# One MLP kernel: blocks of 256 or 320 tokens within a batch instead of blocks of 512 tokens across batches

## The chip, the cores and the metric

The kernel runs on one core of a Trainium2 chip. The metric is the device time of one execution in microseconds (us). Before the change the median of three runs is 1290.62 us (1290.39 to 1291.06).

## The reference

For 8 batches of 576 tokens and 8 heads of 64, an attention over 32 memory slots is followed by two MLP blocks, all in float32:

```
a    = softmax(phi, over the 576 tokens)          # phi: (8, 8, 576, 32)
k_m  = a^T k ;  v_m = a^T v                       # per batch and head: (32, 64)
x    = softmax(q k_m^T / 8) v_m                   # heads joined: (8, 576, 512)
x    = x + relu(layernorm(x) * g1 @ w1) @ w2      # w1: (512, 2048), w2: (2048, 512)
h    = gelu(x @ w_in);  u, v = halves of h        # w_in: (512, 1024)
v_s  = w_sg @ (layernorm(v) * g2) + b_sg          # mixes the 576 tokens of a batch
out  = x + (u * v_s) @ w_out                      # w_out: (512, 512)
```

w1, w2, w_in and w_out arrive as 64-bit words that are converted on the chip.

## The kernel before, in words

Two batches form a pair of 1152 tokens, that is 9 tiles of 128; tile 4 of a pair holds the last 64 tokens of its even batch and the last 64 of its odd batch (`tile_rows`). There are 36 tiles.

**Phase 1** computes attention and the first MLP. Because x is a product of attention weights (256 of them per token) and v_m, the kernel folds w1 into the values: for each batch b and each part fb of 512 of the 2048 hidden columns, `make_vw` (line 507) multiplies the batch's v_m with the centred, scaled w1 (`WC`, read back from a scratch in HBM by `load_wc`) and splits the result into a high and a low float32r half, VW[b, fb]: two tiles of 4 KB per partition. So the weights of the first matmul differ from batch to batch. The attention of a tile (`lay_q`, `load_q`, `t_q`, `t_scores`, `t_norm`, `t_attn`) ends with the transposed attention weights in aT, again as high and low halves; `t_x` computes x itself for the residual, `t_ln` its statistics. Before a batch's first tile come its `load_phi`, `load_kv`, and the `prep_` functions.

The MLP runs over 9 blocks of 512 tokens (4 tiles), each in 16 chunks c of 128 hidden columns; one step is one block and chunk. `m1` (line 549) multiplies VW with aT into the PSUM tile ph: six matmuls (two row halves times high-high, high-low and low-high) for each piece of the block that belongs to one batch (`pieces`, line 537). relu goes by ScalarE (hh, line 563) and VectorE (the low half hl, line 564), on all 512 columns at once. `m2` (line 567) multiplies hh and hl of each of the four tiles with W2[c], three matmuls of 512 columns per tile, accumulated over the 16 chunks in four PSUM banks; LAG = 2 steps lie between m1 and m2. The last block takes its chunks in the order 12 to 15, 0 to 11.

The rest of phase 1 is placed by an event list: `at_time(time, function, ...)` with times in steps (16 per block, `tile_base` for tiles), negative ones before the first step; `run_until` calls what is due in the middle and at the end of a step. The framework's scheduler starts from this program order when it orders each engine's queue. Nearly all DMAs are issued by SyncE in one queue (line 80).

Buffers: wpool has 22 slots of 4 KB per partition (raw weights, the 16 final W2, some VW, later the weights of phase 2, the normalised v tiles vhl and, for pair 0, scratch), wpool2 has 13 (wc and the other VW). ph has two PSUM banks, the y of m2 four, attention two.

**Phase 2** is the second MLP, per pair. Its beginning is laid beside the last block's 16 steps by `begin_phase2(n)`: w_sg, w_in and w_out are loaded and split, `y_in` reads pair 0's tiles back transposed, and `s2` (v half, its gelu and layer norm, into vhl) runs for tiles 0 to 4. Then `phase2` runs `s3` (u half), `s4` (mixing over tokens, pvs), and `s5` (output) in 16 units per pair, with `s2` of pair 0's remaining tiles and of the next pair between them.

Of the kernel before, what the change touches and what calls it, by code (L numbers as in the profile page):

```python
# [28 lines left out]
def fused_kernel(ctx: ExitStack, tc: tile.TileContext, q, k, v, phi, g1, w1, w2, w_in, g2, w_sg, b_sg, w_out, out):  # L29
# [7 lines left out]
    P = 128  # L37
# [6 lines left out]
    B1, F1 = 9.2, 0.5  # L44
    HK = H * NM // P
    BLK = TB * P
    NB = B * S // BLK
    REM = S - 4 * P
    SCALE = 1.0 / math.sqrt(D)
# [23 lines left out]
    wpool = ctx.enter_context(tc.tile_pool(name="wpool", bufs=22))  # L73
# [61 lines left out]
    def phase1():  # L135
        R["mo"] = mo = pool(es_mlp, "mo", 2)
        ps_h = pool(es_mlp, "ps_h", 2, space=PSUM)
        ps_y = pool(es_mlp, "ps_y", 1, space=PSUM)
        at = pool(es_attn, "at", 1, side="right")
        at2 = pool(es_attn, "at2", 2, side="right")  # L140
        ps_a = pool(es_attn, "ps_a", 2, space=PSUM, side="right")
        wpool2 = pool(es_w2, "wpool2", 13)
# [25 lines left out]
        def load_phi(b, gs):  # L168
            if gs[0] == 0:
                st["phi"] = (  # L170
# [3 lines left out]
            ph, pr = st["phi"]  # L174
# [5 lines left out]
        def load_kv(b, g, part):  # L180
            n = 3 * g + part
            if b == 0 and n >= 3:
                t = wpool.tile([P, 2, 4, 2, D], F32, tag="w", name="kv")
            else:
                t = at2.tile([P, 2, 4, 2, D], F32, tag="kv", name="kv", bufs=3)
# [10 lines left out]
            st["kv", g, part] = t  # L196
# [11 lines left out]
        def load_q(u, b, i):  # L208
            n = u["n"]
            if u["T"]["t"] < TB:  # L210
                if i % 2 == 0:
                    st["q0"] = two(wpool, F32, "q0")
                t = st["q0"][i % 2].rearrange("p (h d) -> p h d", h=H)
                load(t, q[b, :, i * P:(i + 1) * P, :].rearrange("h p d -> p h d"))
# [7 lines left out]
        def prep_max(b, gs):  # L222
            ph, pr = st["phi"]
# [14 lines left out]
            st["dg"] = dg  # L238

        def prep_exp(b, gs):  # L240
            ph, pr = st["phi"]
            n, hs = len(gs), slice(4 * gs[0], 4 * gs[-1] + 4)
            mb = ps_of(b, [P, 4 * n, NM], "mb")
            PE.matmul(mb.rearrange("p h m -> p (h m)"), ones, st["dg"].rearrange("p g n -> p (g n)"), start=True, stop=True)
# [5 lines left out]
        def prep_sum(b):  # L250
            ph, pr = st["phi"]
# [12 lines left out]
            st["rs"] = rs  # L264

        def prep_kv(b, g, part):
            ph, pr = st["phi"]
            if (g, part) == (0, 0):
                st["kvp"] = ps_a.tile([P, 2, 2 * D], F32, tag="a", name="kvp")
            kvp = st["kvp"]  # L270
            t = st.pop(("kv", g, part))
# [30 lines left out]
        def prep_kT(b):  # L302
            kvn = st["kvn"]
# [33 lines left out]
        def t_scores(u):  # L337
            n, kT = u["n"], st["kT"]
# [643 lines left out]
```

## Time and profile before

| | |
|---|---|
| median of three runs | 1290.62 us (1290.39 to 1291.06) |
| span of the profiled execution, first to last instruction | 1287.4 us |
| TensorE busy | 1230.4 us |
| VectorE busy | 679.6 us |
| ScalarE busy | 440.6 us |
| GpSimd busy | 408.6 us |
| mean granted clock of TensorE, share of full speed | 0.981 |

The profile is of one execution, and gives no time of its own for it beside the span; the median of the runs is 3.2 us above the span. "Busy" counts the time in which an engine has at least one instruction in work; matmuls overlap each other, so the cost of one is read from the distance between starts and not from its own duration.

### The profile page before, as it was taken

The page shows a single profiled execution, that of the slowest core. Times are in us where ns is not written, and L with a number is a line of the kernel's source. Part 1 is how long each engine was busy: PE and PEld are TensorE (multiplying, and loading weights), DVE is VectorE, ACT ScalarE, POOL GpSimd, SP SyncE. Part 2 cuts the span into 40 slices and gives each one's busy share as a digit, 9 for nine tenths or more (in the row PEclk, how much of TensorE's full clock was granted, in tenths as well). Part 3 has the DMA queues.
Part 4 walks back from the last instruction along what each step waited for, and adds up shares of the span by engine and source line. Part 5 has one row for each costly group of instructions (what it writes and reads, how often), then busy time and mean ns, then how long its engine had stood idle before and what let it go on. Part 6 is the DMA issues. An engine that isn't in the chain of part 4 may idle for free.

```text
span 1287.4 us, 20559 instructions
## 1 busy us (share of the span) xinstructions
PE 1230.4 (96%) x7723; PEld 1024.8 (80%) x7723; DVE 679.6 (53%) x1472; ACT 440.6 (34%) x870; POOL 408.6 (32%) x659
## 2 busy tenths in 40 slices
PE   4589989999999999999999999999999999999998
PEld 2367667888878888788787888778998998998997
DVE  3677564445355355345354434765567547547632
ACT  2653332222223232132132123543353444434430
POOL 1144222111102111111021112514575666647641
PEclk8689989999999999999999999999999999999999
DMA  9996673164353453532431104322033024013301
GB/s 213 305 259 162 188 189 91 52 182 123 100 146 99 117 142 89 146 106 79 136 83 58 51 25 136 123 84 75 25 91 106 1 80 134 9 34 115 91 9 66
DMA packets 205076, 138.96 MB, mean 108 GB/s; under 512 B 95536, under 2 KB 176688, under 8 KB 204976
## 3 DMA queue, kind: packets, MB, share of 16 engines
q1 hardware_dynamic: 204976, 137.64, 38.4%
q8 instruction: 61, 1.00, 0.3%
q14 instruction: 39, 0.32, 0.1%
HBM read 114.53 MB, written 31.46 MB: 113 GB/s over the span
## 4 chain that ended last, share of the span: by engine, by line
PE 84%; DMA 7%; DVE 4%; SPq 2%; issue 1%; ACT 1%; POOL 1%; POOLq 0%; DVEq 0%; ACTq 0%
PE ph L559 17%; PE py L574 9%; PE py L576 9%; PE pvs L891 9%; PE py L575 9%; PE po L914 8%; PE pu L866 7%; PE pv L794 6%; DMA raw<-in_moe_w_ch_dram 4%; PE pvw L515 2%; PE sc L342 2%; SPq L80 2%; PE kvp L276 1%; DMA kv<-in_v_dram 1%; PE px L452 1%
## 5 line engine op out<-in xcount | busy, mean ns | idle before, releaser
L559 PE MATMUL ph<-aTh,vw 128*128 128x64 f32 (+7 forms) x1024 | 254.1, 318 | 10.2 <-ACT aTh L410 4.6
L574 PE MATMUL py<-whl,hh 128*128 128x512 f32 x576 | 230.3, 403 | 0.0
L575 PE MATMUL py<-whl,hh 128*128 128x512 f32 x576 | 227.5, 395 | 0.0
L576 PE MATMUL py<-whl,hl 128*128 128x512 f32 x576 | 225.6, 395 | 0.0
L559 PEld LDWEIGHTS ph<-aTh,vw 128*128 128x128 f32 x1024 | 178.2, 191 | 33.3 <-issue 7.5
L564 DVE SCALAR_TENSOR_TENSOR hl<-ph,hh 128x512 fp32r<-128x512 f32 x144 | 99.0, 687 | 169.8 <-ACT hh L563 169.5
L563 ACT ACTIVATE hh<-ph 128x512 fp32r<-128x512 f32 x144 | 86.0, 599 | 266.2 <-PE ph L559 264.9
L559 PE MATMUL ph<-aTl,vw 128*128 128x448 f32 (+7 forms) x512 | 163.7, 320 | 0.0
L574 PEld LDWEIGHTS py<-whl,hh 128*128 128x128 f32 x576 | 108.6, 188 | 30.0 <-issue 6.3
L576 PEld LDWEIGHTS py<-whl,hl 128*128 128x128 f32 x576 | 108.3, 188 | 27.9 <-issue 5.1
L421 POOL TENSOR_TENSOR z<-z,r 128x256 f32<-128x256 f32 (+1 forms) x36 | 20.5, 570 | 342.7 <-DVE r L420 278.7
L575 PEld LDWEIGHTS py<-whl,hh 128*128 128x128 f32 x576 | 108.6, 189 | 20.9 <-issue 2.1
L891 PE MATMUL pvs<-wsh,vhl 128*128 128x288 f32 x576 | 121.2, 294 | 0.0
L559 PEld LDWEIGHTS ph<-aTl,vw 128*128 128x128 f32 x512 | 97.7, 191 | 16.0 <-issue 8.6
L866 PE MATMUL pu<-yTh,whl 128*128 128x288 f32 x512 | 110.4, 295 | 0.0
L794 PE MATMUL pv<-whl,yTh 128*128 128x512 f32 x288 | 91.9, 400 | 3.8 <-DVE vg L784 3.8
L891 PEld LDWEIGHTS pvs<-wsh,vhl 128*128 128x128 f32 x576 | 94.3, 188 | 0.6
L914 PE MATMUL po<-whl,gh 128*128 128x512 f32 x288 | 90.8, 391 | 0.0
L866 PEld LDWEIGHTS pu<-yTh,whl 128*128 128x128 f32 x512 | 85.0, 188 | 1.0
L866 PE MATMUL pu<-yTl,whl 128*128 128x288 f32 x256 | 75.4, 295 | 0.0
L891 PE MATMUL pvs<-wsl,vhl 128*128 128x288 f32 x256 | 75.4, 295 | 0.0
L894 POOL TENSOR_TENSOR gt<-gt,ug 128x288 f32<-128x288 f32 x64 | 51.6, 808 | 63.7 <-DVE gt L893 62.8
(161 smaller groups left out, 2079.0 us busy)
## 6 DMA issues: line engine op xcount, KB each, us to landing
wc<-w_d SPq DMA_DIRECT2D x56, 512.0 KB, 4.9
y_d<-x SPq DMA_DIRECT2D x36, 256.0 KB, 3.9
yr<-y_d SPq DMA_DIRECT2D x36, 256.0 KB, 3.0
kv<-in_k_dram SPq DMA_DIRECT2D x32, 256.0 KB, 4.3
kv<-in_v_dram SPq DMA_DIRECT2D x32, 256.0 KB, 4.4
raw<-in_moe_w_ch_dram SPq DMA_DIRECT2D x32, 256.0 KB, 9.6
raw<-in_moe_w_ch_dram SPq DMA_DIRECT2D x16, 512.0 KB, 8.2
out_dram<-yr SPq DMA_DIRECT2D x32, 256.0 KB, 2.0
```

The source lines that it names most:

```text
L80: return nc.sync.dma_start(out=out_ap, in_=in_ap)
L559: PE.matmul(ph[:, c0:c1], w[:, ks], x[:, g, c0:c1], start=(n == 0), stop=(n == 3 * HK - 1))
L563: A.activation(hh, ph, AF.Relu)
L564: st["hl"] = V.scalar_tensor_tensor(out=hl, in0=ph, scalar=0.0, in1=hh.bitcast(F32), op0=ALU.max, op1=ALU.subtract)
L574: PE.matmul(py, hh[:, ts_], wh, start=start, stop=False)
L575: PE.matmul(py, hh[:, ts_], wl, start=False, stop=False)
L576: PE.matmul(py, hl[:, ts_], wh, start=False, stop=stop)
L794: PE.matmul(pv, y[:, kc, cs], w, start=(n == 0), stop=(n == 3 * KC - 1))
L866: PE.matmul(pu, w[:, ds_], y[:, kc, cs], start=(n == 0), stop=(n == 3 * KC - 1))
L891: PE.matmul(pvs, v_, w_, start=(n == 0), stop=(n == len(ops) - 1))
L894: G.tensor_tensor(out=gt, in0=gt, in1=ug, op=ALU.mult)
L914: PE.matmul(po, gg[:, dc, cs], w, start=(n == 0), stop=(n == 3 * KC - 1))
```

## The change

- **Blocks.** There are 16 blocks within a batch instead of 9 across batches. An even batch has a block of 256 tokens and then one of 320, an odd batch one of 320 and then one of 256. Every m1 is one piece of six matmuls.
- **Carry.** relu's result for an even batch's last 64 tokens is stored per chunk in a carry tile (16 of them); the odd batch's first block puts its own tokens of tile 4 beside them, and m2 takes that full tile there. relu of a 320-token block is two instructions on each engine instead of one, 64 and 256 columns.
- **Order.** Batch 0 goes part by part of w1 through both blocks; the last batch goes chunk by chunk through both; all others finish one block and then the other. Times in the event list count 18 per batch. LAG is 3 of the shorter steps, and hh and hl have four buffers.
- **Event times.** All tile times and those of W1, W2, `make_vw` and `load_wc` are new.
- **Buffers.** wpool has 19 slots; VW rotates over five places of two tiles; wc has four tiles; kv two instead of three; x seven instead of eight; aT three. In phase 2, vhl of tiles 7 and 8 goes to a new pool w3, and pv has one bank until phase 2 (tile 35's y takes the other).
- **Batch 0's fifth group.** The 64 tokens of tile 4 go through the same functions as the first four tiles, as a third group.

```
-    B1, F1 = 9.2, 0.5
+    F1 = 0.5
...
+    BW = 2 * P + REM
+    VQ = 5
+    VMAIN = (4, 0)
+    VTAIL = 2 * (VQ - len(VMAIN))
+    LAG = 3
...
-    wpool = ctx.enter_context(tc.tile_pool(name="wpool", bufs=22))
+    wpool = ctx.enter_context(tc.tile_pool(name="wpool", bufs=19))
...
+        crp = pool(es_mlp, "crp", 1)
...
-        wpool2 = pool(es_w2, "wpool2", 13)
+        vmain = pool(es_mlp, "vmain", 2 * len(VMAIN))
+        tail = pool(es_w2, "tail", 1)
...
-                t = at2.tile([P, 2, 4, 2, D], F32, tag="kv", name="kv", bufs=3)
+                t = at2.tile([P, 2, 4, 2, D], F32, tag="kv", name="kv")
...
+        def aT_of(j):
+            if j not in aT:
+                aT[j] = tuple(mo.tile([P, HK, BW], F32R, tag=f"aT{n}", name=f"aT{n}", bufs=3) for n in "hl")
+            return aT[j]
...
+        def t_x(u, b):
+            T, o, n = u["T"], u["o"], u["n"]
...
+        def wc_tiles():
+            return [tail.tile([P, 2, DM], F32, tag="wc", name="wc", bufs=4) for _ in range(2)]
...
-                h, l = two(wpool if b % 2 and fb < NFB - 1 else wpool2, F32R, "vw")
+                q_ = (NFB * b + fb) % VQ
+                if q_ in VMAIN:
+                    t = vmain.tile([P, 2, DM], F32R, tag="w", name="vw")
+                else:
+                    t = tail.tile([P, 2, DM], F32R, tag="vw", name="vw", bufs=VTAIL)
...
+        blocks = []
+        for b in range(B):
+            w = 18 * b
+            if b % 2 == 0:
+                blocks += [(b, 0, 2 * P, w, 8), (b, 2 * P, S, w + 8, 10)]
+            else:
+                blocks += [(b, 0, 2 * P + REM, w, 10), (b, 2 * P + REM, S, w + 10, 8)]
...
+        def relu(out_h, out_l, src):
+            A.activation(out_h, src, AF.Relu)
+            return V.scalar_tensor_tensor(out=out_l, in0=src, scalar=0.0, in1=out_h.bitcast(F32), op0=ALU.max, op1=ALU.subtract)
...
         def m1(j, c):
...
-            ph = ps_h.tile([P, BLK], F32, tag="h", name="ph")
-            for c0, c1, b in pieces(j):
-                n = 0
-                for g in range(HK):
-                    wh, wl = VW[b, fb][g]
-                    for w, x in ((wh, ah), (wh, al), (wl, ah)):
-                        PE.matmul(ph[:, c0:c1], w[:, ks], x[:, g, c0:c1], start=(n == 0), stop=(n == 3 * HK - 1))
...
+            ph = ps_h.tile([P, BW], F32, tag="h", name="ph")[:, 0:w]
+            n = 0
+            for g in range(HK):
+                wh, wl = VW[b, fb][g]
+                for w_, x in ((wh, ah), (wh, al), (wl, ah)):
+                    PE.matmul(ph, w_[:, ks], x[:, g, 0:w], start=(n == 0), stop=(n == 3 * HK - 1))
+                    n += 1
+            hh = mo.tile([P, 2 * P], F32R, tag="hh", name="hh", bufs=LAG + 1)
+            hl = mo.tile([P, 2 * P], F32R, tag="hl", name="hl", bufs=LAG + 1)
+            o = 0
+            if w > 2 * P:
+                if b % 2 == 0:
+                    carry[c] = crp.tile([P, 2, P], F32R, tag=f"cr{c}", name="cr")
+                    cs, ps = slice(0, REM), slice(2 * P, w)
+                else:
+                    cs, ps = slice(REM, P), slice(0, REM)
+                    o = REM
+                relu(carry[c][:, 0, cs], carry[c][:, 1, cs], ph[:, ps])
+            st["hl"] = relu(hh, hl, ph[:, o:o + 2 * P])
+            hid[j, c] = [(hh[:, n * P:(n + 1) * P], hl[:, n * P:(n + 1) * P]) for n in range(2)]
+            if o:
+                hid[j, c].insert(0, (carry[c][:, 0, :], carry[c][:, 1, :]))
 
         def m2(j, c, start, stop):
...
+            for t, (hh, hl) in enumerate(hid.pop((j, c)), t0):
+                if t not in ybank:
+                    if t == NPAIR * TPP - 1:
+                        ybank[t] = R["ps"].tile([P, DM], F32, tag="v1", name=f"py{t}")
+                    else:
+                        ybank[t] = ps_y.tile([P, DM], F32, tag=f"y{t % TB}", name=f"py{t}")
+                py = ybank[t]
+                PE.matmul(py, hh, wh, start=start, stop=False)
+                PE.matmul(py, hh, wl, start=False, stop=False)
+                PE.matmul(py, hl, wh, start=False, stop=stop)
...
+        BASES = {0: (-17.5, 0, 0, 0, 10.2, 12.0, 13.5, 16.0, 18.5), 1: (-15, -12, -9, -5.3, -1.4, 4, 8, 11.5, 15)}
+        BASES[2] = (-17, -13.1, -9.2, -5.3, -1.4, 4, 8, 11.5, 15)
+        BASES[3] = (-17, -13.3, -9.6, -5.9, -2.6, 2, 5.2, 8.3, 11.4)
+
         def tile_base(t):
-            j, r = divmod(t, TB)
-            if j == 0:
-                return -17.5 + 6 * (r // 2) + 0.1 * (r % 2)
-            if j == 1:
-                return B1 + r + 0.6 * (r > 0)
-            return 16 * j - 18.1 + 3 * r
+            pair, i = divmod(t, TPP)
+            return 36 * pair + BASES[pair][i] + 0.5 * (pair > 0 and i == 4)
...
-                    vw_at = max(16 * (b - 1) + 4 * fb + 5.5, first + 0.5 + 2 * fb)
-                    at_time(vw_at - (4 if fb == 0 else 1.5), load_wc, fb)
+                    vw_at = 18 * b + ((-12, -6.8, -4.2, -1.7) if b % 2 else (-12, -5.3, -3.3, -1.3))[fb]
+                    vw_at = max(vw_at, first + 0.5 + 2 * fb)
+                    at_time(vw_at - (4 if fb == 0 else 2.5), load_wc, fb)
                     at_time(vw_at, make_vw, b, fb)
...
-            at_time(4 * fb - 18.5 if fb > 1 else 0.3 * fb - 26.5, load_w1, fb)
-            at_time((-16.5, -5.5, 2.6, 6.6)[fb], scale_w1, fb)
-            at_time((-16.4, -0.6, 4.0, 8.0)[fb], center_w1, fb)
-            at_time((-15, 0.8, 5.1, 9.1)[fb], make_vw, 0, fb)
+            at_time((-26.5, -26.2, -2.5, 2.0)[fb], load_w1, fb)
+            at_time((-16.5, -5.0, 3.0, 7.5)[fb], scale_w1, fb)
+            at_time((-16.4, -0.3, 4.6, 9.1)[fb], center_w1, fb)
+            at_time((-15, 1.3, 5.8, 10.3)[fb], make_vw, 0, fb)
         for c in range(NF):
-            at_time(1.1 * c - 16 if c > 2 else 0.2 * c - 26.4, load_w2, c)
-            at_time(1.0 * c - 4 if c < 2 else 1.0 * c - 2.6, split_w2, c)
+            split_at = 4.5 * (c // 4) + 0.5625 * (c % 4) - 0.6 if c > 3 else 0.9 * c - 4
+            at_time(split_at - 5 if c > 3 else -12.7 if c == 3 else 0.2 * c - 26.4, load_w2, c)
+            at_time(split_at, split_w2, c)
...
-        LAG = 2
         LAST = [*range(12, NF), *range(12)]
-        steps = [(j, c if j < NB - 1 else LAST[c]) for j in range(NB) for c in range(NF)]
+        steps = []
+        for b in range(B):
+            js = (2 * b, 2 * b + 1)
+            if b == 0:
+                order = [(j, 4 * fb + n) for fb in range(NFB) for j in js for n in range(4)]
+            elif b == B - 1:
+                order = [(j, c) for c in LAST for j in js]
+            else:
+                order = [(j, c) for j in js for c in range(NF)]
+            if b in (0, B - 1):
...
+            last = n - NF * (len(blocks) - 2)
+            if last % 2 == 1:
+                assert last < 0 or not ev
+                begin_phase2(last // 2)
...
+        R["pv"] = v_ = R.get("p2") and not R.get("pv", 0)
+        pv = R["ps"].tile([P, DM], F32, tag="v1" if v_ else "v0", name="pv")
...
-            vh, vl = two(wpool, F32R, "vhl")
+            vh, vl = two(wpool if t < TPP - 2 else R["w3"], F32R, "vhl")
...
+        R["w3"] = pool(es_left, "w3", 2)
```

## Rows read from the trace of the kernel before

**Rows 1.** The page's table of engines: busy us, share of the span, instructions.

```profile
PE 1230.4 (96%) x7723; PEld 1024.8 (80%) x7723; DVE 679.6 (53%) x1472; ACT 440.6 (34%) x870; POOL 408.6 (32%) x659
```

**Rows 2.** The page's chain of waits, its shares of the span by line.

```profile
PE ph L559 17%; PE py L574 9%; PE py L576 9%; PE pvs L891 9%; PE py L575 9%; PE po L914 8%; PE pu L866 7%; PE pv L794 6%; DMA raw<-in_moe_w_ch_dram 4%; PE pvw L515 2%; PE sc L342 2%; SPq L80 2%; PE kvp L276 1%; DMA kv<-in_v_dram 1%; PE px L452 1%
```

**Rows 3.** Busy time by stretch: length, engines (count), granted clock, DMA share, GB/s.

```profile
56.00:86.00 30.00, 25.20 (x96) 17.96 (x97) 24.98 (x43) 20.41 (x35) 5.69 (x5) 0.79 1.02 296
...
156.00:178.00 22.00, 14.69 (x146) 8.46 (x152) 14.41 (x37) 5.35 (x11) 8.40 (x11) 0.77 0.59 144
...
178.00:778.00 600.00, 598.67 (x4031) 490.16 (x4016) 275.09 (x642) 156.34 (x317) 89.32 (x187) 1.00 0.38 104
...
778.00:893.00 115.00, 108.69 (x501) 88.29 (x500) 73.97 (x144) 51.41 (x110) 40.85 (x56) 0.99 0.38 114
```

**Rows 4.** TensorE in time, five steps: start us, us, line, operation, shape, count.

```profile
849.00 0.40 PE L559 MATMUL ph<-aTh,vw 128*128 128x512 f32 x1
...
850.38 0.39 PE L574 MATMUL py<-whl,hh 128*128 128x512 f32 x1
...
759.86 0.36 PE L559 MATMUL ph<-aTh,vw 128*128 128x448 f32 x1
...
761.97 0.39 PE L575 MATMUL py<-whl,hh 128*128 128x512 f32 x1
...
692.44 0.33 PE L559 MATMUL ph<-aTh,vw 128*128 128x384 f32 x1
...
694.41 0.40 PE L575 MATMUL py<-whl,hh 128*128 128x512 f32 x1
...
597.25 0.30 PE L559 MATMUL ph<-aTh,vw 128*128 128x320 f32 x1
...
597.98 0.40 PE L559 MATMUL ph<-aTh,vw 128*128 128x320 f32 x2
...
599.03 0.39 PE L575 MATMUL py<-whl,hh 128*128 128x512 f32 x1
...
510.36 0.28 PE L559 MATMUL ph<-aTh,vw 128*128 128x256 f32 x1
...
512.03 0.39 PE L575 MATMUL py<-whl,hh 128*128 128x512 f32 x1
```

**Rows 5.** TensorE's waits from 156 to 178 us: us in total, times, longest.

```profile
PE kvp L276 <- DMA kv<-in_v_dram: 4.4, 2, 3.0
PE mb L244 <- DVE vw L522: 2.0, 1, 2.0
```

**Rows 6.** Relu and its like by shape: count, busy us, mean ns, idle before.

```profile
L564 DVE SCALAR_TENSOR_TENSOR hl<-ph,hh 128x512 fp32r<-128x512 f32 x144 | 99.0, 687 | 169.8 <-ACT hh L563 169.5
...
L782 DVE SCALAR_TENSOR_TENSOR z<-z,pu 128x288 f32<-128x288 f32 x64 | 28.9, 452 | 58.4 <-ACT z L781 58.0
...
L563 ACT ACTIVATE hh<-ph 128x512 fp32r<-128x512 f32 x144 | 86.0, 599 | 266.2 <-PE ph L559 264.9 <-PE py L575 0.6
...
L781 ACT ACTIVATE z<-pu 128x288 f32<-128x288 f32 x64 | 26.2, 410 | 45.9 <-PE pu L866 45.8
```

**Rows 7.** TensorE's waits from 180 to 780 us.

```profile
PE kvp L276 <- DMA kv<-in_v_dram: 1.3, 2, 0.8
```

**Rows 8.** TensorE's waits from 780 to 900 us.

```profile
PE pv L794 <- DVE vg L784: 3.8, 3, 2.8
PE ph L559 <- DVE hl L564: 2.5, 3, 1.3
```

**Rows 9.** One tile's chain behind pv in time, first and last instruction.

```profile
873.89 0.59 ACT L781 ACTIVATE vg<-pv 128x512 f32<-128x512 f32 x1
...
881.89 1.29 POOL L812 TENSOR_TENSOR vhl<-vg,vhl 128x512 fp32r<-128x512 f32 x1 [1.31 <-ACT vhl L811]
```

**Rows 10.** Wc loads (count, KB, us to landing); one pvw group in time.

```profile
wc<-w_d SPq DMA_DIRECT2D x56, 512.0 KB, 4.9
...
311.64 1.09 PE L515 MATMUL pvw<-wc,vT 64*32 64x512 f32 x16
```

More of the change, by code (lines that the diff above doesn't have):

```diff
@@ L484, in scale_w1 @@
         def scale_w1(fb):
-            WC[fb] = ws = [wpool2.tile([P, 2, DM], F32, tag="w", name="wc") for _ in range(2)]
+            WC[fb] = ws = wc_tiles()
             for j, raw in enumerate(raws.pop(fb)):
@@ L501, in load_wc @@
         def load_wc(fb):
-            WC[fb] = [wpool2.tile([P, 2, DM], F32, tag="w", name="wc") for _ in range(2)]
+            WC[fb] = wc_tiles()
             for n in range(2):
                 last = load(WC[fb][n], w_d[fb][:, 2 * n:2 * n + 2, :])
-            st["wc"] = last.ins.name
+            st["wc", fb] = last.ins.name
         def make_vw(b, fb):
@@ L532, in split_w2 @@
             W2[c] = split([raws.pop(("w2", c))], wpool, gate=gate)
-        hid, ybank = {}, {}
-        def pieces(j):
-            out = []
-            for n in range(TB):
-                for o, m, b, _ in tile_rows(*divmod(TB * j + n, TPP)):
-                    c0 = n * P + o
-                    if out and out[-1][2] == b:
-                        out[-1][1] = c0 + m
-                    else:
-                        out.append([c0, c0 + m, b])
-            return out
+        hid, ybank, carry = {}, {}, {}
@@ new lines, in phase1, with where @@
+        blocks = []
[5 more added lines that the diff above has]
+                blocks += [(b, 0, 2 * P + REM, w, 10), (b, 2 * P + REM, S, w + 10, 8)]
+        def where(b, s):
+            return next((j, s - t0) for j, (b_, t0, t1, _, _) in enumerate(blocks) if b_ == b and t0 <= s < t1)
+        def relu(out_h, out_l, src):
+            A.activation(out_h, src, AF.Relu)
+            return V.scalar_tensor_tensor(out=out_l, in0=src, scalar=0.0, in1=out_h.bitcast(F32), op0=ALU.max, op1=ALU.subtract)
@@ L654, in phase1 @@
                 at_time(base + 3 * f, t_attn, u)
[L655 to L658 removed]
+                at_time(base + 4.5, t_x, u, b)
+                if tt % 2 == 1 and (i < 4 or odd):
+                    at_time(base + 4.7, t_ln, tiles[tt - 1:tt + 1])
         ev.sort(key=lambda e: (e[0], e[1]))
@@ L680, in phase1 @@
+        ends = [s_[0] for s_ in steps[1:]] + [18 * B + 0.56 * n for n in range(LAG + 1)]
+        firsts = {j: next(c for _, j_, c in steps if j_ == j) for j in range(len(blocks))}
+        lasts = {j: [c for _, j_, c in steps if j_ == j][-1] for j in range(len(blocks))}
         for n in range(len(steps) + LAG):
+            t0, t1 = ends[n - 1] if n else 0.0, ends[n]
             if n < len(steps):
-                m1(*steps[n])
-            run_until(n + 0.5)
+                m1(*steps[n][1:])
+            run_until((t0 + t1) / 2)
```

194 lines of the change are left out of this document (88 added, 106 removed).

## The prediction, made before the changed kernel was run

> **What bounds the kernel now.** I read the engine table first: TensorE holds a matmul for 96% of the 1287.4 us span, VectorE for 53%, ScalarE for 34% and GpSimd for 32% [rows 1]. By itself 96% says little, because it averages over stages; so I went to the chain of waits, whose largest share is one line, the first MLP matmul m1 (line 559) with 17%, followed by the three lines of the second, m2, with 9% each [rows 2]. Then the stretches [rows 3]. From 178 to 778 us TensorE is busy for 598.67 of 600 us at the full clock, with VectorE at 275 and ScalarE at 156: this stage is worth exactly what its matmuls cost. Around it lie three weaker stretches: 56 to 86 us (transfers at a share of 1.02, VectorE 24.98 of 30, clock 0.79), 156 to 178 us (TensorE 14.69 of 22, clock 0.77), and 778 to 893 us, where the second phase is prepared beside the last block. From 893 us on nothing of the change's loops runs.
>
> So there are four places: the matmuls of the steady stage, the start, the gap at 156 us, and the seam at 778 us.
>
> **1. The matmuls of m1.** The count does not change: before, 2 blocks with 6 and 7 with 12 per chunk, 96 x 16 = 1536; after, 16 blocks x 16 chunks x 6 = 1536. Columns don't change either. What changes is how they are cut: before, pieces of 64 to 512 columns where a batch ends inside a block; after, only 256 and 320. The price is the distance from the start of the first m1 matmul to the start of the second m2 matmul, less 0.23 us, the pitch of one 512-column matmul (849.00 to 850.38 is six of them) [rows 4]. Taking the second one counts the late start that follows small pieces. 512: 1.38 us. 448+64: 761.97 - 759.86 - 0.23 = 1.88. 384+128: 694.41 - 692.44 - 0.23 = 1.74. 320+192: 599.03 - 597.25 - 0.23 = 1.55. 256+256: 512.03 - 510.36 - 0.23 = 1.44. A piece of 64 thus costs far more than its columns: 1.88 for the same 512 columns that take 1.38 in one piece.
> Blocks 0 and 8 are 512, 1 and 7 448+64, 2 and 6 384+128, 3 and 5 320+192, 4 is 256+256: 2 x (1.38 + 1.88 + 1.74 + 1.55) + 1.44 = 14.54 us per chunk, x16 = 232.6.
> After, per batch and chunk: 256 costs 1.44 / 2 = 0.72; 320 has five pitches from 597.25 to 597.98, 0.146 each, so 0.88. 1.60 x 16 x 8 = 204.8. The gain is 27.8 us, nearly all of it in the stage where TensorE is the bound: **-28**. Block by block the pitches vary by a hundredth of a microsecond per step; I keep -26 to -30.
> m2 has 36 tiles x 16 x 3 = 1728 matmuls before and after, with the same shape (the odd 64 tokens wait in the carry until the next batch fills their tile): 0. In t_x the mixed tile had two groups of six matmuls, and has two groups of 64 tokens now: 0.
>
> **2. The gap at 156 to 178 us.** TensorE's queue stands behind kv matmuls that wait 4.4 us for their transfer, and a ones-matmul that waits 2.0 [rows 5]; with half clock in between, 22 us hold some 7 us of work. Both belong to batch 2's preparation, which the event list puts at 11.4 to 16.9 (units of one step), right where batch 1's tiles 5 to 7 (bases 10.8 to 12.8) are wanted for block 1 at 16. After, batch 2's tiles begin at 36 - 15 = 21, so its preparation starts at 15.5, and batch 1's first block (tiles 4 to 6, 320 tokens) is due at 18 with its last attention step at 13.5 + 2.1. So the two preparations pull 4 units apart, and less of batch 1 is due. Against it: kv has two buffers instead of three, and SyncE's one queue still takes phi, kv, q and weights in order. Bounds: all 15 us go; or the wait moves with batch 2 and the tighter kv buffers add one landing, +4. I take **-9**, nearer to the lower end because nothing of batch 1's second block is due before 28.
>
> **3. The start.** The first m1 needs VW(0,0) and two tiles. Five q tiles and a third small score group (64 tokens) are added to VectorE's and ScalarE's queues ahead of it, and relu gets dearer while VectorE is busy 83% of 56 to 86 us [rows 3]. From the rows, VectorE's relu takes 687 ns for 512 columns, and 452 for 288 in the same kind of operation: 1.05 ns a column, so 418 for 256 and 217 for 64. ScalarE: 599 and 410, so 383 and 221 [rows 6]. These are estimates; no row has 256 or 64. One chunk of batch 0 costs VectorE 2 x 418 + 217 = 1053 ns, where 576 columns cost 773 before: four or five chunks, +1.4 us, and the third group about as much. Against it, the W1 and W2 loads from the third part on are issued later in the list, so fewer conversions stand ahead of VW(0,1). Bounds -3 to +6; I take **+2**. The interleaving of blocks 0 and 1 itself buys 576 - 512 = 64 tokens more of m1 per part of W1, under 0.25 us a chunk: nothing.
>
> **4. Less slack behind each step.** ph has two buffers. Before, two m2 (12 x 0.23 each) and an m1 lie between a step's end and the reuse of its ph: 2 x 2.76 + 1.6 = 7.1 us. After: 2 x 1.38 + 0.8 = 3.6. hh has four buffers with a lag of three steps, 3 x (1.38 + 0.8) = 6.5 us instead of 2 x 4.4 = 8.7. What must fit is ScalarE's and VectorE's relu of one step: 221 + 383 + 418, and for VectorE's queue whatever stands there. In all VectorE gets 256 x 0.418 + 128 x 0.217 - 99.0 = +36 us and ScalarE 256 x 0.383 + 128 x 0.221 - 86.0 = +40, over some 780 us: VectorE goes from 46% to about 51% in the steady stage. Today TensorE waits there for 1.3 us in all, and only for kv [rows 7]. I take **+3**; from 0 to +10 (0.04 us for each of the 256 steps).
> [...]
>
> **5. The seam, 778 to 893 us and after.** TensorE waits here for the pv chain (3.8 us) and for hl (2.5) [rows 8]. The last batch now brings 576 x 16 tokens of work beside the same conversions (1.60 + 15 x 0.23 = 5.05 us per chunk, not 4.14), which covers more of them. But pv has one bank until the second phase (tile 35's y takes the other); and wpool has 19 slots, while pair 0 wants 12 weights + 7 normalised tiles + 1 scratch = 20: tile 6's vhl must wait until the batch-0 half of s4 has freed slots, and tiles 7 and 8 follow it. One tile's chain, from the first Square at 873.89 to vl's end at 881.89 + 1.29, takes 9.3 us [rows 9]; two or three in a row are 14 to 20 us, against which TensorE has four s5 (12 x 0.23 = 2.8 us each) and two s3, about 14 us. Bounds -6 (both waits gone) to +8. I take **+2**.
>
> **Sum.** 1287.4 - 28 - 9 + 2 + 3 + 2 = 1257.4 us. The profiled span lies 3.2 us under the median of the runs, 1290.62; I add that back: **1261 us** (1260.6).
>
> **The rivals.**
> (a) The gap moves instead of closing: batch 2's kv comes late again, with two buffers, and the same 9 us are lost at the end of batch 0. For it: the single SyncE queue. Against: 4 units more distance. 1261 + 9 = 1270.
> (b) The halved slack bites: 0.06 us on each of 256 steps, 15 us instead of 3, and the seam at its bad end: 1261 + 12 + 4 = 1277. For it: VectorE's single instructions of 1 to 2 us in a ring of 3.6. Against: no wait for hl in the steady stage now.
> (c) Start, gap and seam all close: -15, 0, 0, -4 instead of -9, +2, +3, +2: 1261 - 17, about 1244 to 1250.
> (d) m1's cost is linear in columns, so that cutting differently gains nothing: 1290.6 - 9 + 7 = 1288.6. The rows speak against it: 512 columns take 1.38, 1.44, 1.55, 1.74 and 1.88 us, depending on the cut. [...]
> (e) Slower: the ring of five VW parts. The next batch's part 1 can be written only when this batch's last block has read part 0, so the weights of a batch are made in its predecessor's last 7 units. If a boundary exposes the chain, it costs the wc load of 4.9 us, one pvw group of 1.1, and a copy and a subtraction of 512 columns, taken as relu's 0.60 + 0.69 [rows 6, 10]: 7.3 us, at seven boundaries 51: 1261 + 51 = 1312. It decides from 30 / 7 = 4.3 us per boundary. Against: the list makes part 1 at least 5 units, over 25 us, before it is read, and part 3 is read 6 units in, except in the last batch.
>
> **How the numbers follow.** Forecast 1255 to 1267: 0.42. (a) 0.18, (b) 0.17, (c) 0.13, (d) 0.03, (e) with the seam gone wrong 0.07. A measurement of this kernel tells 0.2%, 2.6 us, from no change; so faster 0.90, same 0.03, slower 0.07. The range of 1245 to 1283 leaves out (d), (e) and the far ends of (b) and (c).
>
> **What would show it.** Right: no m1 matmul of 64 to 192 columns; groups of six at 0.72 and 0.88 us; m1's total busy time down by over 25 us; TensorE without waits over 1 us between the first two batches and in the steady stage. Step 2 is wrong if TensorE again waits for kv between batches 0 and 2; 4 if waits for relu's output sum to over 10 us; 5 if pvs waits for vhl. If VW's copies release m1 at each batch boundary, (e) holds, and the prediction fails.

## The result: 1257.2 us, 2.5% faster, as forecast and a little more

The changed kernel takes **1257.17 us** (median of 4 runs, 1255.38 to 1258.34), the kernel before 1290.51 us beside it; the ratio is 0.975, 95% interval 0.9735 to 0.9765. The forecast was 1261, with 1245 to 1283 as its range. Run a second time, the changed kernel gave 1257.18 us and a ratio of 0.9744 (0.9730 to 0.9758). The profiled execution has a span of 1253.6 us, before 1287.4.

The page after: first the table of engines, then the chain of waits by line.

```profile
PE 1207.7 (96%) x7727; PEld 1003.1 (80%) x7727; DVE 702.8 (56%) x1713; ACT 476.0 (38%) x1111; POOL 406.9 (32%) x657
```

```profile
PE ph L580 14%; PE pvs L946 9%; PE py L609 9%; PE py L611 9%; PE py L610 9%; PE pu L921 8%; PE po L969 8%; PE pv L851 7%; SPq L83 3%; DMA raw<-in_moe_w_ch_dram 2%; PE pvw L526 2%; PE sc L348 2%; PE kvp L282 2%; DMA phi<-in_phi_dram 1%; PE px L460 1%
```

Beside [rows 1, 2]: TensorE is as full as before (96%) of a shorter span, VectorE and ScalarE carry 23 and 35 us more. In the chain m1 (line 559 before, 580 now) falls from 17% to 14%, and the transfer of raw weights from 4% to 2%; m2 and the second phase keep their shares within a point.

The same four stretches as [rows 3] (length, busy us of TensorE, its weight loads, VectorE, ScalarE, GpSimd, granted clock, DMA share, GB/s):

```profile
56.00:86.00 30.00, 30.00 (x153) 22.75 (x153) 22.83 (x48) 21.57 (x43) 9.36 (x10) 0.95 0.89 239
156.00:178.00 22.00, 15.80 (x95) 12.93 (x90) 15.93 (x41) 6.82 (x16) 5.62 (x9) 0.84 0.64 165
178.00:778.00 600.00, 599.69 (x4071) 480.35 (x4070) 317.38 (x888) 200.83 (x553) 102.25 (x205) 1.00 0.42 115
778.00:893.00 115.00, 110.18 (x628) 96.61 (x627) 68.27 (x151) 46.90 (x104) 48.32 (x73) 1.00 0.18 52
```

From 56 to 86 us TensorE is now full (25.20 to 30.00 us of 30, clock 0.79 to 0.95). The gap at 156 us is still there: 15.80 busy of 22, before 14.69.

**Where the 33.8 us came from.** For every matmul I took the distance from its start to the next one's start. Summed by line, m1 falls from 246.1 to 217.7 us (-28.4), m2 rises from 419.7 to 427.7, the preparation and attention of the batches with the wait ahead of the first matmul fall from 195.3 to 183.4, and the second phase from 422.2 to 420.6. A sum by line puts a wait on the line ahead of it, so I also subtracted each kind's undisturbed distance (the mean of the middle 80% of its distances after 180 us, by line and shape, from both traces). This splits the span into clean work and time lost, that is waits and the longer distances where the granted clock is lower (in the kernel before, m1's 512-column matmuls start 0.427 us apart from 57 to 61 us, at a clock of 0.50, and 0.229 at the full clock):

```
                              before    after   difference
clean: m1                      230.8    204.2     -26.6
clean: all other matmuls       909.4    909.9      +0.5
lost, 0 to 86 us                63.9     54.5      -9.4
lost, 86 to 156 us              11.7     17.0      +5.3
lost, 156 to 178 us             14.2      9.7      -4.5
lost, 178 to 697 us             41.6     42.9      +1.3
lost, 697 us to last matmul     11.8     11.3      -0.5
```

The last 4 us, from the start of the last matmul to the end of the span, are nearly the same in both and are left out.

The stretches are the same times in both traces, so some work shifts over an edge; what is lost inside a stretch is still where the trace shows it. The prices of kinds that run only before 180 us have to be guessed, so the first two stretches are good to about 1 us.

m1's undisturbed distances by columns are, at the full clock, 64: 0.104, 128: 0.107, 192: 0.110, 256: 0.119, 320: 0.146, 384: 0.178, 448: 0.208, 512: 0.229 us. TensorE in time, one step of each kind in the changed kernel (start us, us, line, operation, shape, count):

```profile
430.70 0.28 PE L580 MATMUL ph<-aTh,vw 128*128 128x256 f32 x1
...
431.41 0.63 PE L611 MATMUL py<-whl,hl 128*128 128x512 f32 x2
...
403.61 0.30 PE L580 MATMUL ph<-aTh,vw 128*128 128x320 f32 x1
...
404.49 0.39 PE L611 MATMUL py<-whl,cr 128*128 128x512 f32 x1
```

431.41 - 430.70 = 0.71 and 404.49 - 403.61 = 0.88 us: the forecast had 0.72 and 0.88, worked out from steps of other sizes [rows 4].

The relu by shape (count, busy us, mean ns, idle before), which [rows 6] did not have:

```profile
L567 DVE SCALAR_TENSOR_TENSOR hl<-ph,hh 128x256 fp32r<-128x256 f32 x256 | 106.4, 420 | 103.7 <-ACT hh L566 102.1
L567 DVE SCALAR_TENSOR_TENSOR cr<-ph,cr 128x64 fp32r<-128x64 f32 x128 | 28.3, 221 | 50.9 <-ACT cr L566 49.9
L566 ACT ACTIVATE hh<-ph 128x256 fp32r<-128x256 f32 x256 | 97.0, 384 | 145.2 <-PE ph L580 94.0 <-DVE cr L567 45.9 <-DVE mv L470 3.2
L566 ACT ACTIVATE cr<-ph 128x64 fp32r<-128x64 f32 x128 | 28.6, 223 | 96.4 <-PE ph L580 96.1
```

The estimates were 418, 217, 383 and 221 ns; measured are 420, 221, 384 and 223. Relu alone thus costs VectorE 106.4 + 28.3 - 99.0 = +35.7 us and ScalarE +39.6 (forecast +36 and +40).

TensorE's waits (engine, line, what it waits for: us in total, times, longest), from 156 to 178 us, then from 180 to 780, then the three longest from 780 to 900, as [rows 5, 7, 8]:

```profile
PE px L460 <- DVE vw L538: 3.3, 1, 3.3
PE pvw L526 <- issue: 2.9, 1, 2.9
```

```profile
PE kvp L282 <- DMA kv<-in_v_dram: 0.2, 1, 0.2
```

```profile
PE ptw L791 <- issue: 2.2, 1, 2.2
PE pv L851 <- DVE vg L840: 1.0, 2, 0.8
PE py L609 <- ACT hh L566: 0.6, 2, 0.4
```

In the gap TensorE no longer waits for batch 2's kv, but for VectorE's work on batch 1. In the steady stage it waits for next to nothing (0.2 us), and at the seam the waits for vg and hl (3.8 and 2.5) have shrunk to 1.0 and none (0.5 us for the other relu of VectorE, cr); no wait of pvs for vhl is listed.

### The profile page after: what moved, and what is told of

It is laid out like the page before. It is cut to its first block, busy times and chain, and to the rows that moved or that the text cites. A ratio compares the mean times of both kernels' runs of the same rounds, so it can differ in the third digit from the quotient of the medians.

```text
span 1253.6 us, 21085 instructions
## 1 busy us (share of the span) xinstructions
PE 1207.7 (96%) x7727; PEld 1003.1 (80%) x7727; DVE 702.8 (56%) x1713; ACT 476.0 (38%) x1111; POOL 406.9 (32%) x657
## 4 chain that ended last, share of the span: by engine, by line
PE 82%; DMA 6%; DVE 4%; SPq 3%; issue 3%; POOL 1%; ACT 1%; DVEq 0%; POOLq 0%; ACTq 0%
PE ph L580 14%; PE pvs L946 9%; PE py L609 9%; PE py L611 9%; PE py L610 9%; PE pu L921 8%; PE po L969 8%; PE pv L851 7%; SPq L83 3%; DMA raw<-in_moe_w_ch_dram 2%; PE pvw L526 2%; PE sc L348 2%; PE kvp L282 2%; DMA phi<-in_phi_dram 1%; PE px L460 1%
## 5 line engine op out<-in xcount | busy, mean ns | idle before, releaser
L580 PE MATMUL ph<-aTh,vw 128*128 128x320 f32 (+1 forms) x1024 | 249.8, 305 | 5.5 <-ACT vw L537 3.7
L609 PE MATMUL py<-whl,hh 128*128 128x512 f32 x512 | 205.5, 404 | 1.7 <-ACT hh L566 1.7
L610 PE MATMUL py<-whl,hh 128*128 128x512 f32 x512 | 202.0, 395 | 0.0
L611 PE MATMUL py<-whl,hl 128*128 128x512 f32 x512 | 185.8, 397 | 0.0
L567 DVE SCALAR_TENSOR_TENSOR hl<-ph,hh 128x256 fp32r<-128x256 f32 x256 | 106.4, 420 | 103.7 <-ACT hh L566 102.1
L580 PE MATMUL ph<-aTl,vw 128*128 128x256 f32 (+1 forms) x512 | 153.6, 300 | 0.0
L566 ACT ACTIVATE hh<-ph 128x256 fp32r<-128x256 f32 x256 | 97.0, 384 | 145.2 <-PE ph L580 94.0
L609 PEld LDWEIGHTS py<-whl,hh 128*128 128x128 f32 x512 | 96.5, 189 | 31.6 <-issue 7.3
L610 PEld LDWEIGHTS py<-whl,hh 128*128 128x128 f32 x512 | 96.7, 189 | 18.6 <-issue 0.7
L611 PEld LDWEIGHTS py<-whl,hl 128*128 128x128 f32 x512 | 91.7, 190 | 13.6 <-issue 2.4
```

Source lines behind the costliest of these rows:

```text
L566: A.activation(out_h, src, AF.Relu)
L567: return V.scalar_tensor_tensor(out=out_l, in0=src, scalar=0.0, in1=out_h.bitcast(F32), op0=ALU.max, op1=ALU.subtract)
L580: PE.matmul(ph, w_[:, ks], x[:, g, 0:w], start=(n == 0), stop=(n == 3 * HK - 1))
L609: PE.matmul(py, hh, wh, start=start, stop=False)
L610: PE.matmul(py, hh, wl, start=False, stop=False)
L611: PE.matmul(py, hl, wh, start=False, stop=stop)
```

## The experiments

Times are medians; every ratio is to the kernel before, run on the same chip. "Lost" is the sum defined above.

**1. The price of small pieces, taken away from the kernel before (b_uncut).**

```
-            for c0, c1, b in pieces(j):
+            for c0, c1, b in [(0, BLK, pieces(j)[-1][2])]:
```

> The kernel before, with m1 of every block in one piece of 512 columns: where two batches share a block, the weights of the later batch serve all of it (left out: the earlier batch's weights for its columns; 864 matmuls of m1 instead of 1536, the columns are the same). Theory (a piece has a price beside its columns): all 9 blocks cost 1.38 us a chunk, 9 x 16 x 1.38 = 198.7 us instead of 232.6, so -34 us: about 1257, and a little lower if the waits for a new batch's weights go too. Rival (the cost is linear in columns): 0, about 1290. Between them: if only about half of it shows, the small pieces were partly hidden behind other waits of TensorE.

Measured: 1272.39 us, ratio 0.9858 (0.9834 to 0.9881): -17, half of what was expected, in the middle between theory and rival. m1's own distances fell nearly as said, 246.1 to 215.6 us (-30.5). But the time lost from 178 to 697 us rose from 41.6 to 55.6. TensorE's five largest waits from 178 to 778 us in this kernel:

```profile
PE pvw L515 <- issue: 5.9, 2, 3.4
PE kvp L276 <- DMA kv<-in_v_dram: 2.0, 2, 1.8
PE pvw L515 <- ACT aTh L439: 1.9, 1, 1.9
PE ph L559 <- ACT aTh L439: 1.9, 2, 1.4
PE px L452 <- ACT aTh L439: 1.6, 1, 1.6
```

They and one of 1.3 us sum to 14.6 us, against 1.3 us in all [rows 7]: with shorter m1 in the old order of work, TensorE comes too early for the cast that ends the attention chain (aTh) and for pvw, with which the next batch's weights begin, and half the gain turns into waits. (For the largest of these the profile names no releaser; experiments 5 to 7 show one for the wait ahead of pvw in the changed kernel.) So the price isn't linear in the columns, and the larger pieces bring their full gain only if the rest of the list fits them. In the changed kernel it does: 0.2 us of waits there. This kernel leaves out the earlier batch's weights and so has 672 matmuls fewer, which the changed kernel hasn't; part of its gain is theirs, and the distances by size given above are the better evidence for the price of a small piece.

**2. Small pieces put back into the changed kernel (a_cut64).**

```
+                for c0, c1 in [(0, REM), (REM, w)] if b % 2 and w > 2 * P else [(0, w)]:
...
-                        PE.matmul(ph, w_[:, ks], x[:, g, 0:w], start=(n == 0), ...)
+                        PE.matmul(ph[:, c0:c1], w_[:, ks], x[:, g, c0:c1], start=(n == 0), ...)
```

> The changed kernel, with the 320-column blocks of the odd batches cut into 64 + 256 columns in m1, same output. 4 batches x 16 chunks = 64 steps. Theory: a 64-column group of six with its late start costs what it cost before, 1.88 - 1.38 + 64 columns' share (0.03 x 6) = about 0.5 us a step beyond the one piece, so +30 to +36 us: about 1290. Rival (linear in columns): 0 to +2, about 1258.

Measured: 1292.86 us, ratio 1.0026 (1.0015 to 1.0037): +35.7, at the upper end, and with it all of the change's gain is gone. m1's distances rise from 217.7 to 250.0. One step in time:

```profile
400.06 0.19 PE L581 MATMUL ph<-aTh,vw 128*128 128x64 f32 x1
400.08 0.28 PE L581 MATMUL ph<-aTl,vw 128*128 128x64 f32 x1
...
400.85 0.28 PE L581 MATMUL ph<-aTl,vw 128*128 128x256 f32 x1
...
401.44 0.40 PE L610 MATMUL py<-whl,cr 128*128 128x512 f32 x1
```

1.38 us for the 320 columns that take 0.88 in one piece, 0.50 more, x64 = 32 us. The rest of the 35.7 lies mostly at the seam (10.9 us lost from 778 to 900 us, 6.7 in the changed kernel). The linear rival is out: by columns alone the step would have stayed at 0.88.

**3. Batch 0's two blocks in the other order (a_rev0).**

```
-                order = [(j, 4 * fb + n) for fb in range(NFB) for j in js for n in range(4)]
+                order = [(j, 4 * fb + n) for fb in range(NFB) for j in js[::-1] for n in range(4)]
```

> The changed kernel, with batch 0's two interleaved blocks in the other order in each step: the block of tiles 2 to 4 (320 tokens) ahead of the block of tiles 0 and 1 (256). Theory: the early first m1 (48.3 us, before 56.2) comes from its needing two tiles only; then the first m1 now comes 4 to 8 us later, at 52 to 56, and the total rises by 3 to 7 us, to 1260 to 1264. Rival: the earlier start comes from the order of transposes and small tiles (q cut in two) whatever block is first; then first m1 stays within 2 us and the total within 1 us.

Measured: 1263.44 us, ratio 0.9788 (0.9765 to 0.9811): +6.3. TensorE in time around the first m1 matmul, in the kernel before, the changed one, and this one:

```profile
48.47 3.06 PE L515 MATMUL pvw<-wc,vT 64*32 64x512 f32 x16 [6.34 <-DVE wc L498]
56.16 1.22 PE L559 MATMUL ph<-aTh,vw 128*128 128x512 f32 x2 [4.62 <-ACT aTh L410]
```

```profile
42.30 3.06 PE L526 MATMUL pvw<-wc,vT 64*32 64x512 f32 x16 [1.31 <-DVE wc L509]
48.32 0.50 PE L580 MATMUL ph<-aTh,vw 128*128 128x256 f32 x2 [2.96 <-ACT vw L537]
```

```profile
41.99 3.06 PE L526 MATMUL pvw<-wc,vT 64*32 64x512 f32 x16 [1.31 <-DVE wc L509]
55.16 0.90 PE L580 MATMUL ph<-aTh,vw 128*128 128x320 f32 x2 [10.10 <-ACT aTh L416]
```

The brackets are the wait ahead and what ended it. With the block of tiles 0 and 1 first, m1 waits only for the weights (ScalarE's copy of vw); with the block of tiles 2 to 4 first, it waits 10.1 us for their transposed attention. Time lost up to 86 us: 63.9 before, 54.5 changed, 58.8 here. So some 4.3 us of the 9.4 gained there come from a first block that needs two tiles. The rest goes with the weights' chain, which itself starts 6 us earlier (pvw at 42.3, before 48.5); that stays here too. Most of this is VectorE's queue. The first two lines are of the kernel before, the third of the changed one:

```profile
38.43 3.70 PE L496 MATMUL cm<-wc,mean 128*128 128x512 f32 x8
...
47.21 2.34 DVE L498 TENSOR_TENSOR wc<-wc,cm 128x1024 f32<-128x1024 f32 x2
```

```profile
41.02 2.35 DVE L509 TENSOR_TENSOR wc<-wc,cm 128x1024 f32<-128x1024 f32 x2 [0.73 <-PE cm L507]
```

The centring of the weights (wc) comes 5.1 us after cm's last matmul in the kernel before, behind the softmax of the first tiles, which VectorE works on from 43.26 to 46.95 us, and follows cm at once in the changed one. Which of the new event times brings this order wasn't tested.

**4. Batch 0 not interleaved (a_plain0).**

```
-                order = [(j, 4 * fb + n) for fb in range(NFB) for j in js for n in range(4)]
+                order = [(j, c) for j in js for c in range(NF)]
```

(and the loads and conversions of W1, W2 and VW at earlier times in the list)

> The changed kernel, with batch 0's two blocks one after the other, not interleaved; the loads and conversions of W1, W2 and the VW parts are put earlier in the list to suit. Prediction's view: interleaving blocks 0 and 1 buys nothing, so 0 to +2 us: 1257 to 1259. Rival: with 256 tokens a part of W1 must last 4 steps of 2.1 us instead of 8, and TensorE waits for the conversions of W1 and W2 on VectorE and ScalarE: +8 to +20 us, 1265 to 1277, lost between 50 and 100 us of the span.

Measured: 1281.24 us, ratio 0.9919 (0.9891 to 0.9947): +24. TensorE's three longest waits from 46 to 135 us:

```profile
PE ph L580 <- DVE hl L567: 9.3, 2, 5.4
PE ph L580 <- ACT vw L537: 7.5, 4, 2.4
PE py L609 <- ACT whl L121: 2.8, 2, 2.4
```

The rival holds in kind, but the loss is 4 us above its upper end, and not all of it lies where it was expected: against the changed kernel 13 us more are lost up to 86 us and 9 more from 86 to 156, but also 8 more from 178 to 697, while the gap loses 7 less. The expectation also puts the prediction's sentence wrongly: it compared interleaved blocks (576 tokens a part) with the old first block (512), and against that the gain is small indeed. What it missed is that 256-token blocks without the interleaving, in the list tried here, cost most of what the cut gives.

**5 to 7. The gap at 156 us: q's buffer, batch 1 earlier, both (a_q2, a_early1, a_q2early); a_again is the standard.**

```
-                t = at.tile([P, 4 * DM // 16, 4], F32, tag="q", name="q")...
+                t = at.tile([P, 4 * DM // 16, 4], F32, tag="q", name="q", bufs=2)...
```

```
-        BASES = {0: (-17.5, 0, 0, 0, 10.2, 12.0, 13.5, 16.0, 18.5), ...
+        BASES = {0: (-17.5, 0, 0, 0, 8.7, 10.5, 12.0, 14.5, 17.0), ...
```

> The changed kernel again, as the standard beside the next three on the same chip: 1255 to 1259 us, ratio to before 0.9735 to 0.9765.

> The changed kernel with two buffers for the incoming q tile instead of one. In its trace TensorE loses 2.9 us at 159.8 us (pvw) and 3.3 us at 163.8 us (px, for VW's subtraction), and ahead of both VectorE's queue stands behind a transpose that waits for a q tile landing at 161.1 us, whose load could go out only when the single buffer had been read at 157.7 us. Theory: with a second buffer this landing is no longer waited for, and 3 to 5 us of the 6.2 go: 0.3% faster than the standard. Rival: the attention chain of batch 1 (scores, reduce, normalise, transpose, cast) is itself that late, or the one DMA queue is: 0.

> The changed kernel with the attention work of batch 1 put 1.5 units (of 4.9 us: some 7 us) earlier in the list. Theory (this chain is late for batch 1's first block): the loss of 6.2 us between 159 and 168 us shrinks by 3 to 5 us. Rival: the wait moves forward with the work, into the stretch before 156 us, where VectorE is no freer (49.9 us busy of 70): 0 +- 1.

> Both of these together. If q's buffer and the lateness are two separate causes: -5 to -6 us against the standard, 1251 to 1252. If they are one cause: the larger of the two alone.

Measured: a_again 1257.18 (ratio 0.9744); a_q2 1257.97 (0.9756, 0.9740 to 0.9772); a_early1 1263.81 (0.9793, 0.9778 to 0.9808); a_q2early 1264.04 (0.9801, 0.9788 to 0.9815). Lost from 156 to 178 us: 10.9, 9.2, 2.1, 2.2; from 86 to 156 us: 16.0, 17.9, 31.5, 34.4. TensorE's waits from 156 to 178 us with two q buffers, then the longest from 96 to 178 us with batch 1 earlier:

```profile
PE px L460 <- DVE vw L538: 3.3, 1, 3.3
PE pvw L526 <- issue: 2.6, 1, 2.6
```

```profile
PE kvp L282 <- DMA kv<-in_v_dram: 10.8, 4, 4.3
```

The transpose of q on VectorE in the standard and with two buffers:

```profile
161.79 1.08 DVE L338 STREAM_TRANSPOSE qT<-q 128x512 f32<-128x512 f32 x1 [1.73 <-DMA q<-q_d]
```

```profile
162.77 1.04 DVE L338 STREAM_TRANSPOSE qT<-q 128x512 f32<-128x512 f32 x1
```

My theory of q's buffer falls: with two buffers VectorE no longer waits for the landing, and TensorE's two waits (2.6 and 3.3) are as in the changed kernel (2.9 and 3.3). VectorE is simply at work there, one instruction behind another (idle for 1.5 us in all from 158.1 to 169.1 us with two buffers), on tile 6's scores, the two y additions of batch 0's end and VW's subtraction. With all of batch 1 earlier the gap closes, so it is batch 1's work in VectorE's queue that is late; but its kv preparation, which hangs on the same times, moves with it, and TensorE waits 10.8 us for kv. That is a wait of the kind of [rows 5] in another place. The total is 6.6 us worse, and with both edits it is the same as with this one alone.

For the first wait, ahead of pvw, the profile names no releaser, but VectorE's queue shows one. `make_vw` lets pvw's matmuls start only behind two small memsets on VectorE. The second one in the changed kernel:

```profile
162.57 0.06 DVE L522 MEMSET pvw<- 128x2 f32 x1
```

pvw starts at 162.74. In a_again, a_q2 and a_t56 the memset starts at 163.15, 164.09 and 161.43 us and pvw at 163.31, 164.25 and 161.59, each 0.16 us later. In experiment 1, where the waits of 3.4 and 2.5 us ahead of pvw have no releaser either, the one of 1.3 us has this memset (line 511 there) as its releaser by name. The memset itself is short, but stands in the queue behind the y additions and tile 6's scores. So some 3 us of the gap hang on a place in the queue; moving the memset wasn't tried.

**8. Only the late tile earlier (a_t56).**

```
-        BASES = {0: (-17.5, 0, 0, 0, 10.2, 12.0, 13.5, 16.0, 18.5), ...
+        BASES = {0: (-17.5, 0, 0, 0, 10.2, 11.75, 12.4, 16.0, 18.5), ...
```

> The changed kernel, with only tile 6 (1.1 units, some 5 us) and tile 5 (0.25 units) of batch 1 earlier in the list; tile 4, and with it the whole preparation of batch 1 (kv, kT, VB), stays where it was. When everything of batch 1 was moved 1.5 units, the loss between 156 and 178 us fell from 9.7 to 2.1 us, but 8 waits for kv of 13.9 us in all came in ahead of it. Theory (the gap is tile 6's chain being late; the kv waits came from the preparation, moved into the time of the W1 and W2 loads): the kv waits stay at about 3.3 us, the gap loses 3 to 5 us: 1252 to 1254. Rival: tile 6's q layout and landing collide with the kv loads as well: no gain, 1257 to 1260.

Measured: 1254.11 us, ratio 0.9726 (0.9712 to 0.9739): 3 us below the changed kernel, the fastest of all, though the interval overlaps that of the standard (0.9730 to 0.9758). The waits for kv stay at 2.9 us in all, and the gap shrinks from two waits of 2.9 and 3.3 (4.5 and 2.4 in the standard) to

```profile
PE pvw L526 <- issue: 2.3, 1, 2.3
PE ph L580 <- ACT aTh L446: 2.3, 1, 2.3
```

The time lost from 156 to 178 us is 8.3 (9.7 and 10.9), 1.4 to 2.6 us less where 3 to 5 were expected. This agrees with the theory in kind; the gain is at its low end or below, and whether it is real rests on the trace more than on the measured time.

**9. Less slack (a_lag2) and more (a_t56lag4).**

```
-    LAG = 3
+    LAG = 2
```

> The changed kernel with m2 two steps behind m1 instead of three (three buffers of hh and hl instead of four), so that the time from relu to m2's need falls from 6.5 to 4.4 us. Step 4 of the prediction (halved slack costs +3 us, 0 to +10): if any slack is being used up now, another cut shows it at 0.01 to 0.04 us a step: +3 to +10, with waits of m2 for hh or hl. If slack is no term at all: 0 +- 1.

Measured: 1266.73 us, ratio 0.9825 (0.9809 to 0.9841): +9.5, at the upper end. Lost against the standard: +3.0 up to 156 us, +1.5 from 178 to 697, +2.2 from 697 to 778, +4.1 to 900. TensorE's two longest waits from 690 to 880 us:

```profile
PE py L609 <- ACT cr L566: 3.8, 2, 2.3
PE ph L580 <- DVE hl L567: 2.4, 3, 1.4
```

So slack is paid where VectorE and ScalarE have other work, at both ends, and hardly in the steady stage. The other direction, on top of experiment 8:

```
-    LAG = 3
+    LAG = 4
...
-                T["x"] = mo.tile([P, DM], F32, tag="x", name="x", bufs=7)
+                T["x"] = mo.tile([P, DM], F32, tag="x", name="x", bufs=6)
```

> The kernel with tiles 5 and 6 of batch 1 earlier (1254.1 us), with m2 four steps behind m1 instead of three (five buffers of hh and hl; the room for them is taken from x, six tiles instead of seven). Two steps behind cost 9.6 us. Theory A (the slack of three steps is just enough; the forecast's +3 for it is not there): four steps give 0 to -1.5 us, 1252.5 to 1254.5. Theory B (step 4's +3 is in the time of the changed kernel, beside gains elsewhere): -2 to -5 us, 1249 to 1252. The six x tiles can cost: then waits of px's copy or of y's write show, +1 to +5.

Measured: 1268.66 us, ratio 0.9839 (0.9817 to 0.9861). From 178 to 697 us the loss is 42.1, against 41.9 with three steps: theory A, there is nothing more to get in the steady stage. Most of the 14.6 us by which the total rises is lost from 697 to 778 us (16.8, against 5.3 in experiment 8), and the trace puts it on the other edit. ScalarE and then VectorE in time (the bracket is the idle time ahead and what ended it):

```profile
737.41 0.59 ACT L463 COPY x<-px 128x512 f32<-128x512 f32 x1 [5.28 <-DMA y_d<-x]
```

```profile
738.03 0.69 DVE L469 BATCH_NORM_STATS2 s<-x 128x6 f32<-128x512 f32 x1 [2.41 <-ACT x L463]
738.73 0.06 DVE L522 MEMSET pvw<- 128x2 f32 x1
```

The copy into x waits for a y tile to be written out, VectorE's statistics wait for the copy, and the 0.06 us memset that releases TensorE's pvw stands behind them: TensorE waits 4.4 us there, and 4.2 us more for VW's subtraction. Since both edits are in one kernel, only the stretch before 697 us speaks on slack.

**10. The last batch not interleaved (a_plain7).**

```
-                order = [(j, c) for c in LAST for j in js]
+                order = [(j, c) for j in js for c in LAST]
```

> The changed kernel with the last batch's two blocks one after the other instead of interleaved. Each part of W2 and VW is then read for the last time 8 steps later at the earliest (in the second block), so the slots that phase 2's weights need come free in the last 16 steps of 2.3 us only (37 us, instead of 80). Theory: split and load of the second phase's weights are late, TensorE waits for pv's operands at the seam: +10 to +30 us, with waits of pv for whl and a first pv after 840 us (792 now). Rival (the seam has slack, as the forecast's +2 was not seen): 0 to +3.

Measured: 1266.99 us, ratio 0.9818 (0.9803 to 0.9832): +9.8, just below the low end of the theory, and not by its mechanism: the first pv comes at 805.8 (792.3) and no wait of pv for whl is listed. The loss from 778 us on is 17.4 us, against 6.7. TensorE's four longest waits from 780 to 900 us:

```profile
PE py L609 <- ACT hh L566: 3.6, 4, 1.4
PE pv L851 <- DVE vg L840: 1.3, 2, 0.7
PE pvs L946 <- POOL vhl L869: 1.3, 2, 0.7
PE pvs L946 <- ACT vhl L868: 1.3, 1, 1.3
```

From 800 to 820 us ScalarE and GpSimd are busy for 14.83 and 16.44 of 20 us (6.03 and 6.39 in the changed kernel): the conversions come in a crowd beside the last block. TensorE waits 3.6 us for relu's hh, and pvs now does wait for vhl.

## Why the prediction was right, step by step

The sum was -30 us on the span (1287.4 to 1257.4); the trace gives -33.8. The forecast counted m2's late start after small pieces with m1, the table above counts it as lost. So step 1 is priced here as the forecast did it, by the median of the undisturbed steps after 180 us in both traces: 512 columns take 1.36 us, 448+64 1.88, 384+128 1.73, 320+192 1.55 and 256+256 1.44, in the changed kernel 256 take 0.72 and 320 take 0.88; in all 232.0 before and 204.0 after. The 1.4 us beyond the -26.6 of the table are taken from the steady stage's loss:

```
step                        forecast   measured
1  m1's matmuls                -28       -28.0   (-26.6 - 1.4)
2  gap at 156 us                -9        -4.5
3  start, up to 156 us          +2        -4.1   (-9.4 + 5.3)
4  slack, 178 to 697 us         +3        +2.7   (+1.3 + 1.4)
5  seam, from 697 us            +2        -0.5
   other clean work              0        +0.5
```

**Step 1** holds: m1's matmuls have 256 or 320 columns and its groups the forecast price. Experiment 2 shows it from the other side: put small pieces back and all 2.5% is gone. One of the signs named for it was badly chosen. m1's busy time, all lines together (length, busy us of matmuls and of weight loads, clock, DMA share, GB/s), before and after:

```profile
0.00:1300.00 1300.00, 270.69 (x1536) 235.31 (x1536) 0.98 0.38 107
```

```profile
0.00:1300.00 1300.00, 254.31 (x1536) 228.17 (x1536) 0.99 0.39 107
```

It falls by 16.4 us, not by "over 25". Busy spans of pipelined matmuls overlap (a 256-column one is busy 0.28 us and the next starts after 0.119), so the time in which any of them is busy is no price; the start-to-start distance is.

**Step 2** was mis-sized, at half. Its picture of the old cause was right: batch 2's kv is no longer waited for. But it took the waits away without asking firmly enough what is late next: VectorE's queue with batch 1's attention and, in it, the memset that pvw waits for. Experiment 6 shows this, experiment 8 in part; experiment 6 also shows why the list can't just be shifted. The sign of being right, no wait over 1 us between the first two batches, failed (2.9 and 3.3 us), with another cause than rival (a) named.

**Step 3** had the wrong sign. It counted what is added to VectorE's and ScalarE's queues ahead of the first m1. It said that the first m1 needs two tiles, but gave no price to their having been four; in the kernel before that wait is 4.6 us for aTh (experiment 3). It also left out that the centring of the first weights no longer stands behind the softmax. 5.3 us of the gain are given back by 156 us; 3.3 of them are one wait of TensorE between 86 and 156 us, for VectorE's maximum of phi (pt behind pm), which the kernel before doesn't have there.

**Step 4** holds in size. TensorE's waits for relu sum to 1.5 us at the seam and 4.3 us in the whole span, short of the 10 that would have refuted it. Experiment 9 tells what the prediction could not: three steps of lag are about the least, two cost 9.5 us, four give nothing in the steady stage. Rival (b) was thus one step of lag away, and would have struck at the two ends.

**Step 5** came out 2.5 us better. No wait for vhl appears, though the slots are one short by the prediction's count; whether more of them would bring anything wasn't tried. Rival (e), the ring of five VW parts, doesn't show: from 180 to 780 us TensorE's waits sum to 0.2 us.

Two errors of opposite sign, +4.5 in the gap and -6.1 in the start, nearly cancel. That is luck: the total is better than its terms, of which steps 1 and 4 came out as reckoned.

## What to carry to other kernels

Price a cut of TensorE's work by the distance from one start to the next for each size, not by columns or by busy time: here a piece of 64 columns cost nearly as much as one of 192 (0.104 and 0.110 us a matmul). Such a gain on the bounding engine arrived here only with the producers' order moved to fit it: larger pieces in the old order gave half, and the two interleavings were worth 24 us (first batch, with its event times) and 10 us (last batch). Where a wait is removed, look at what else was due at that moment, and at what a step shifted earlier will collide with.

## What the hardware showed that I had not expected

Matmuls of m1 with 64, 128 and 192 columns start 0.104, 0.107 and 0.110 us apart, at the full clock and each with a weight load of its own (1536 loads for 1536 matmuls), while 256 columns take 0.119 and 512 take 0.229: from 64 to 192 columns the distance hardly depends on the size. The records' busy time doesn't tell (in experiment 2's step the second matmul of 64 columns is busy for 0.28 us, and so is one of 256).

A wait that the trace names last need not be the one to remove: with q's landing gone, VectorE's queue released TensorE no sooner (waits of 2.9 and 3.3 us in the changed kernel, 2.6 and 3.3 with two buffers). And the instruction that holds TensorE up can be a very short one: a 0.06 us memset far back in VectorE's queue kept TensorE waiting for 2.3 to 4.5 us in the gap of four traces.
